# Attention, dense layer and routed experts in one kernel: routing logits in four column groups, shorter routing, weight splits and scores at other steps

## The chip, the cores and the metric

The kernel runs on one core of a Trainium2 chip. The metric is the time on the device in microseconds, as the median of several runs; the time before is 1757.74 us.

## What is computed

The reference, cut to what matters here (`a` below is the output of a two-step attention on packed keys, reshaped to 4608 tokens of 512 values):

```python
h = a @ w_in                        # 4608x512 by 512x2048
x = (h - tanh(h)) @ w_out           # 4608x512: the tokens that are routed
logits = x @ w_gate                 # 512x8
noise_scale = log1p(exp(x @ w_noise))
noisy = logits + noise_scale * noise
top2 = two largest of the 8 per token; weights = softmax over the two
for e in range(8):                  # for the tokens that chose expert e
    out[mask] += weight * (relu(x[mask] @ w1[e]) @ w2[e])
```

## The kernel before

The kernel has three phases. Phase A (about the first 150 us) makes the packed values of the attention. Phase B works on 16 chunks of 288 tokens (`TN`); a batch is two chunks. Phase C runs the experts on blocks of 128 gathered tokens: each block has 12 products of 512 columns for each half of `g1` (L1104) and 24 for `g2` (L1146).

Large products are made of three: both operands are split into a high part in `fp32r` and the rest (`split`, L97 on ACT and L101 on DVE), and high x high, high x low and low x high are added up in PSUM.

Phase B is a loop over 256 steps of 16 to a chunk (numbered 0 to 15 below). A step computes one 128-row piece of the hidden layer, `g1` (L475, 6 products into `h`), its tanh (L482 on ACT) and difference (L484 on DVE, `g`), the split of the piece of the step before into `gh` (L97) and `gl` (L101), and, three steps late, the second product `g2` (L500, 12 products into `acc`). So a step has 18 products of 288 columns. `h` has two PSUM buffers: the products of a step wait until `g` of two steps earlier is made. All other work is hung on these steps by a table (`todo`, filled by `at(t, f)`): at the end of a step its entries are issued in the order in which they were entered, and PE, ACT, DVE and SP run their instructions in the order of issue. POOL is ordered by the scheduler. The entries that matter here:

- `u_mm`, `u_hi`, `u_lo`: four times in an odd chunk, at steps 7, 9, 11 and 15, eight float32 products of 512 columns into `u` and their split.
- Scores of the next chunk (`Queries`): float32 products `sq` (L299), two transposes `st` on DVE, the maximum `mq` (L311), a subtraction on POOL (L315), exponential, sum `rq` (L324 to L326), a multiplication on POOL (L330), a transpose `a` and its split. They start at step 1 of each chunk.
- `rows` and `xsplit` at steps 3 to 6: a finished chunk `xr` is transposed into `row` (L515) for its store, and split into `xh` and `xl`.
- `logits` at step 7 or 13: 4 + 4 `fp32r` products into `lg` (L528, L530), copied to `lgs` (L532). The split of the gate weights stands beside them in 32 columns. `logits_t` one step later: three transposes into `lt` (L544), and an addition of the two halves into `lgt`.
- `route`, once for two chunks, in pieces over some 15 steps from step 9 of an even chunk: small DVE operations on 96x48 values: a polynomial (L583, L584), two maxima, and a running count of tokens for each expert (`Mc`, `msum`, L619, L620). `rank` at step 13 of the next odd chunk: two products (L629, L630); then `slots`, and 12 scatters on POOL.
- `load_w`, `split_w`, `store_w` for 128 pieces `wt` of the expert weights: 256 KB loaded by SP, split by ACT and DVE, 512 KB stored by SP. They were spread evenly, load 4 steps ahead of the split and store one step behind it. `wt` has four buffers, so a load waits for the store four pieces earlier. The steps of the splits:

```python
j = T0 + (217 - T0) * i // 128
at(max(T0 - 1, j - 2), load_w, i)
at(j + 2, split_w, i)
at(j + 3, store_w, i)
```

The PSUM pool `pm` (tag `m`, two buffers) is shared by `u`, `sq`, `lg`, `lt` and `rk`. The last chunk's split, logits and routing stand in the first blocks of phase C (`run`, through `L`).

Of the kernel before, what the change touches and what calls it, by code (L numbers as in the profile page):

```python
# [21 lines left out]
P = 128  # L22
# [329 lines left out]
def consts_b(K, pp, pq, zero, w_gate, w_noise):  # L352
# [14 lines left out]
    wraw = pp.tile([P, 4, 16], F32, name="wgraw")  # L367
    nc.sync.dma_start(wraw[:, :, :8], w_gate.rearrange("(c p) e -> p c e", p=P))
    nc.sync.dma_start(wraw[:, :, 8:], w_noise.rearrange("(c p) e -> p c e", p=P))
    K.wg = cp.tile([P, 4, 32], FR, name="wg")  # L370
    nc.vector.tensor_copy(K.wg[:, :, :16], wraw)
    nc.vector.tensor_tensor(K.wg[:, :, 16:], wraw, K.wg[:, :, :16].bitcast(F32), op=ALU.subtract)
# [18 lines left out]
def phase_b(K, stack, wo_stack, qT, w1, w2, w_out, wide_out, noise, w_gate, w_noise, out):  # L391
# [25 lines left out]
    with ExitStack() as ctx:  # L417
# [99 lines left out]
        def xsplit(ch, d):  # L517
            xr = XT[ch]
            if d == 0:
                RAW["xs", ch] = tuple(xp.tile([P, 4, TN], FR, tag=f"x{x}", name=f"x{x}{ch}") for x in "hl")  # L520
            xh, xl = RAW["xs", ch]
            split(K, xh[:, d], xl[:, d], xr[:, d], "act", "dve")
# [17 lines left out]
        def logits_t(ch):  # L540
            lgs = RAW.pop(("lgs", ch))
            lt = pm.tile([P, 512], F32, tag="m", name=f"lt{ch}")
            for i in range(3):
                nc.tensor.transpose(lt[:96, i * 32:(i + 1) * 32], lgs[:, i * 96:(i + 1) * 96], K.ident[:32, :32])  # L544
            if ch % 2 == 0:
                LG[ch // 2] = rt.tile([96, 6, 16], F32, tag="lg", name=f"lgt{ch}")
            z = LG[ch // 2][:, (ch % 2) * 3:(ch % 2) * 3 + 3, :]
            ltv = lt[:96, :96].rearrange("p (i n) -> p i n", i=3)
            nc.vector.tensor_copy(z, ltv[:, :, :16])
            nc.vector.tensor_tensor(z, ltv[:, :, 16:], z, op=ALU.add)  # L550
# [12 lines left out]
        def route(u):  # L563
# [52 lines left out]
            Mb, Mc = T("Mb", dt=BF), T("Mc", dt=BF)  # L616
# [6 lines left out]
            RT[u] = (Mb, Mc, m1, m2, o1, o2)  # L623

        def rank(u):
            Mb, Mc, m1, m2, o1, o2 = RT.pop(u)
            n = 8 * u[2]
            rk = pm.tile([P, 512], F32, tag="m", name=f"rk{u[0]}_{u[1]}")
            nc.tensor.matmul(rk[:96, :n], K.tri, Mb.rearrange("p i e -> p (i e)"), start=True, stop=False)  # L629
# [709 lines left out]
```

## Time and profile before

| | |
|---|---|
| runs | 1751.29, 1757.74, 1761.91 us, median 1757.74 |
| the profiled execution: its time, its span | 1761.15 us, 1759.4 us |
| mean granted TensorE clock | 0.959 of full speed |
| PE busy | 1634.9 us, 93% of the span |
| DVE busy | 1201.5 us, 68% |
| ACT busy | 880.8 us, 50% |
| POOL busy | 567.0 us, 32% |
| phase B's steps | 151.1 us to 855 us of the span |

Busy time of PE is the union of its products' spans, and products overlap, so a short wait of PE hides in it; the distance from the start of one product to the start of the next (0.13 us for 288 columns) is what tells them. "Idle before, releaser" at a row's end names the operation whose end let an engine go on.

### The profile page before, as it was taken

To read this page: it belongs to the slowest core of one execution; us is meant where nothing else is said; L and a number is where in the kernel's file an instruction comes from. 1 tells how busy PE (TensorE), PEld (TensorE's weight loads), DVE (VectorE), ACT (ScalarE), POOL (GpSimd) and SP (SyncE) were. 2 spreads that over 40 slices of the span, in tenths; PEclk is the share of its full clock that TensorE was granted. 3 is DMA by queue.
4 is the path that set the end of the run, shared out by engine and by line. 5 is a ranking of instruction groups with operands and counts; after the bars stand their busy time and mean duration, and the time that the engine had idled before them with its cause. 6 is when DMAs were issued, how large, how long until landed. Compare 5 with 4: busy or idle time off the path is not lost.

```text
span 1759.4 us, 29416 instructions
## 1 busy us (share of the span) xinstructions
PE 1634.9 (93%) x9944; PEld 1383.9 (79%) x9944; DVE 1201.5 (68%) x3113; ACT 880.8 (50%) x1876; POOL 567.0 (32%) x559
## 2 busy tenths in 40 slices
PE   5668999999999999999876899999999999999996
PEld 3335889898989898989765688888888888888885
DVE  7886978887878788967464566666666666666652
ACT  3454655555555555544252455555555555555552
POOL 0001200121212121122445544545444454545421
PEclk8677999999999999999898899999999999999998
DMA  8783367777767687833236665523663236722621
GB/s 273 239 273 102 113 215 238 220 244 209 245 208 240 207 246 213 249 76 111 82 81 254 214 214 164 149 49 81 207 235 53 49 81 207 239 49 48 213 57 26
DMA packets 145655, 293.60 MB, mean 167 GB/s; under 512 B 19682, under 2 KB 69130, under 8 KB 140380
## 3 DMA queue, kind: packets, MB, share of 16 engines
q1 hardware_dynamic: 121676, 252.17, 43.1%
q0 software_dynamic: 23824, 39.51, 12.3%
q8 instruction: 80, 1.31, 0.3%
q14 instruction: 75, 0.61, 0.1%
HBM read 687.34 MB, written 107.59 MB: 452 GB/s over the span
## 4 chain that ended last, share of the span: by engine, by line
PE 81%; DVE 10%; ACT 3%; issue 3%; DMA 1%; another core or an unknown queue 1%; POOL 0%; DVEq 0%; POOLq 0%; ACTq 0%
PE ph L1104 23%; PE py L1146 22%; PE acc L500 19%; PE h L475 10%; PE u L441 2%; PE s L175 2%; ACT ht L1126 1%; PE tp L199 1%; PE pv L211 1%; DVE xl L101 1%; DVE g L484 1%; PE sq L299 1%; DVE gl L101 1%; DVE nm L180 1%
## 5 line engine op out<-in xcount | busy, mean ns | idle before, releaser
L1104 PE MATMUL ph<-w0s,xh 128*128 128x512 f32 x1200 | 379.6, 398 | 19.5 <-ACT xh L97 12.9
L1126 ACT ACTIVATE ht<-h 32x256 f32<-32x256 f32 x624 | 259.8, 416 | 266.8 <-issue 139.2
L1146 PE MATMUL py<-w1s,hh 128*128 128x512 f32 x1200 | 373.0, 392 | 3.5 <-issue 3.4
L965 POOL DMA_INDIRECT x<-x1d,gidxm x276 | 265.0, 960 | 320.1 <-DVE xt L975 249.0
L500 PE MATMUL acc<-gh,wol 128*128 128x288 f32 x1024 | 302.7, 296 | 3.0 <-issue 3.0
L500 PE MATMUL acc<-gh,woh 128*128 128x288 f32 x1024 | 302.3, 295 | 2.2 <-issue 2.2
L500 PE MATMUL acc<-gl,woh 128*128 128x288 f32 x1024 | 301.8, 295 | 2.7 <-issue 2.7
L1106 DVE STREAM_TRANSPOSE h<-ph 128x512 f32<-128x512 f32 x150 | 107.3, 716 | 269.8 <-PE ph L1104 239.8
L1104 PEld LDWEIGHTS ph<-w0s,xh 128*128 128x128 f32 x1200 | 228.4, 191 | 72.2 <-ACT xh L97 13.9
L1146 PEld LDWEIGHTS py<-w1s,hh 128*128 128x128 f32 x1200 | 226.6, 189 | 55.1 <-issue 6.8
L1146 PE MATMUL py<-w1s,hl 128*128 128x512 f32 x600 | 235.6, 393 | 8.3 <-DVE hl L1135 6.1
L1104 PE MATMUL ph<-w0s,xl 128*128 128x512 f32 x600 | 238.7, 398 | 0.0
L665 POOL DMA_INDIRECT table<-d,qi x96 | 91.6, 954 | 386.9 <-DVE g L484 227.4
L500 PEld LDWEIGHTS acc<-gh,woh 128*128 128x128 f32 x1024 | 193.5, 189 | 4.8 <-issue 4.8
L500 PEld LDWEIGHTS acc<-gl,woh 128*128 128x128 f32 x1024 | 193.2, 189 | 2.4 <-issue 2.4
L500 PEld LDWEIGHTS acc<-gh,wol 128*128 128x128 f32 x1024 | 193.1, 189 | 1.6 <-issue 1.6
L97 ACT ACTIVATE gh<-g 128x288 fp32r<-128x288 f32 x256 | 113.5, 443 | 153.2 <-DVE g L484 150.2
L1124 DVE TENSOR_SCALAR ht<-h 32x256 f32<-32x256 f32 x576 | 178.5, 310 | 10.6
L475 PE MATMUL h<-a2h,uh 128*128 128x288 f32 x512 | 158.9, 310 | 7.5 <-DVE g L484 6.5
L482 ACT ACTIVATE t<-h 128x288 f32<-128x288 f32 x256 | 103.9, 406 | 113.0 <-PE h L475 94.3
L475 PE MATMUL h<-a2h,ul 128*128 128x288 f32 x512 | 151.6, 296 | 0.2 <-DVE ul L450 0.2
L475 PE MATMUL h<-a2l,uh 128*128 128x288 f32 x512 | 151.5, 296 | 0.0
(234 smaller groups left out, 2468.2 us busy)
## 6 DMA issues: line engine op xcount, KB each, us to landing
w0s<-wsp SPq DMA_DIRECT2D x140, 2048.0 KB
w1s<-wsp SPq DMA_DIRECT2D x140, 2048.0 KB
wsp<-wt SPq DMA_DIRECT2D x128, 512.0 KB
wt<-in_w_dram SPq DMA_DIRECT2D x128, 256.0 KB
kT<-in_kT_dram SPq DMA_DIRECT2D x16, 608.0 KB
out_dram<-zero SPq DMA_DIRECT2D x37, 256.0 KB
v<-in_v_dram SPq DMA_DIRECT2D x16, 576.0 KB
q<-in_qT_dram SPq DMA_DIRECT2D x32, 288.0 KB
```

What stands on the lines that cost most here:

```text
L97: nc.scalar.activation(hi, src, AF.Copy)
L101: e.tensor_tensor(lo, src, hi.bitcast(F32), op=ALU.subtract)
L475: nc.tensor.matmul(h[:, :TN], u[:, G, fs], x[:, G, :], start=(n == 0), stop=(n == 5))
L482: nc.scalar.activation(t, h[:, :TN], AF.Tanh)
L500: nc.tensor.matmul(ACC[ch][d][:, :TN], w[:, d * P:(d + 1) * P], x, start=(f == 0 and n == 0), stop=(f == 15 and n == 2))
L665: ins = nc.gpsimd.indirect_dma_start(out=K.table, out_offset=IO(ap=qi[:, i:i + 1], axis=0), in_=d[:, i, :], in_offset=None, oob_is_err=True)
L965: g = K.nc.gpsimd.indirect_dma_start(out=x[:, b, :], out_offset=None, in_=rows, in_offset=IO(ap=gidx[:, c, b:b + 1], axis=0))
L1104: K.nc.tensor.matmul(p, xx[:, d * P:(d + 1) * P], w[:, fc, ws, d, :], start=(n == 0), stop=(n == 11))
L1106: self.last = V.transpose(h[:, 2 * fc:2 * fc + 2].rearrange("p g n -> p (g n)"), p).ins
L1124: V.tensor_scalar(dst, src, 0.0, None, op0=ALU.max)
L1126: K.nc.scalar.activation(dst, src, AF.Relu)
L1146: K.nc.tensor.matmul(p, xx[:, f * P:(f + 1) * P], w[:, f // 4, ws, f % 4, :], start=(n == 0), stop=(n == 23))
```

## The change

The logits become four float32 products, one for each 128 rows of the contraction, that write four groups of 32 PSUM partitions from the unsplit `xr`; the three transposes become three float32 products with a matrix `fold` that adds the four groups up. The split of `x` goes away. The polynomial takes one operation for two. The running count over six rows is made by the ranking products instead (six more small products for each `rank`, less one) and one reduction. Scores start at step 4 instead of 1. Each entry of the table may carry a weight for DVE, and the splits of expert weights are put by a dynamic program on the 128 steps of least weight among 17 to 218, at most four in a row, with the load three steps ahead instead of four.

```diff
+    K.fold = cp.tile([P, 16], F32, name="fold")
+    nc.vector.tensor_reduce(K.fold, K.ident.rearrange("p (j n) -> p n j", n=16), axis=AX.X, op=ALU.add)
...
-    K.wg = cp.tile([P, 4, 32], FR, name="wg")
...
+    K.wg = cp.tile([P, 4, 32], F32, name="wg")
+    nc.vector.memset(K.wg, 0.0)
+    nc.sync.dma_start(K.wg[:, :, :8], w_gate.rearrange("(c p) e -> p c e", p=P))
+    nc.sync.dma_start(K.wg[:, :, 8:16], w_noise.rearrange("(c p) e -> p c e", p=P))
...
-        def xsplit(ch, d):
...
         def logits(ch):
-            xh, xl = RAW.pop(("xs", ch))
             lg = pm.tile([P, 512], F32, tag="m", name=f"lg{ch}")
             for d in range(4):
-                nc.tensor.matmul(lg[:32, :TN], K.wg[:, d, :], xh[:, d], start=(d == 0), stop=False)
-            for d in range(4):
-                nc.tensor.matmul(lg[:16, :TN], K.wg[:, d, :16], xl[:, d], start=False, stop=(d == 3))
-            lgs = RAW["lgs", ch] = rt.tile([32, TN], F32, tag="lgs", name=f"lgs{ch}")
-            nc.vector.tensor_copy(lgs, lg[:32, :TN])
+                nc.tensor.matmul(lg[32 * d:32 * d + 32, :TN], K.wg[:, d, :], XT[ch][:, d], start=True, stop=True)
+            lgs = RAW["lgs", ch] = rt.tile([P, TN], F32, tag="lgs", name=f"lgs{ch}")
+            nc.vector.tensor_copy(lgs, lg[:, :TN])
...
-                nc.tensor.transpose(lt[:96, i * 32:(i + 1) * 32], lgs[:, i * 96:(i + 1) * 96], K.ident[:32, :32])
+                nc.tensor.matmul(lt[:96, i * 16:(i + 1) * 16], lgs[:, i * 96:(i + 1) * 96], K.fold, start=True, stop=True)
...
-            V.tensor_scalar(acc, s2, 2.0 / 17, 2.0 / 15, op0=ALU.mult, op1=ALU.add)
-            for k in (13, 11, 9, 7, 5, 3):
-                V.tensor_tensor(acc, acc, s2, op=ALU.mult)
-                V.tensor_scalar(acc, acc, 2.0 / k, None, op0=ALU.add)
-                yield
-            V.tensor_tensor(acc, acc, s2, op=ALU.mult)
+            V.tensor_scalar(acc, s2, 2.0 / 17, None, op0=ALU.mult)
+            for k in (15, 13, 11, 9, 7, 5, 3):
+                V.scalar_tensor_tensor(acc, acc, 2.0 / k, s2, op0=ALU.add, op1=ALU.mult)
+                if k % 4 == 3:
+                    yield
...
-            for i in range(n):
-                V.tensor_copy(Mc[:, i], K.msum)
-                V.tensor_tensor(K.msum, K.msum, M[:, i], op=ALU.add)
-                if i % 2:
-                    yield
+            V.tensor_copy(ms, K.msum)
+            yield
+            V.tensor_reduce(Mc, M.rearrange("p i e -> p e i"), axis=AX.X, op=ALU.add)
+            V.tensor_tensor(K.msum, K.msum, Mc, op=ALU.add)
...
-            nc.tensor.matmul(rk[:96, :n], K.ones[:, :96], Mc.rearrange("p i e -> p (i e)"), start=False, stop=True)
+            for j in range(1, n):
+                nc.tensor.matmul(rv[:, j:], K.ones[:, :96], Mb[:, :n - j], start=False, stop=False)
+            nc.tensor.matmul(rv, K.ones[:, :96], ms.unsqueeze(1).to_broadcast([96, n, 8]), start=False, stop=True)
...
-            q = (4, 5, 5, 6, 7, 8, 9, 10, 11, 12) if ch == 1 else (1, 2, 2, 3, 4, 5, 6, 7, 10, 12)
-            at(0 if ch == 1 else w - 3, Q.load_q, ch)
+            q = (4, 5, 6, 7, 8, 9, 10, 11, 12, 13)
+            at(0 if ch == 1 else w - 1, Q.load_q, ch)
...
-                r, pace = {11: (18, 2), 13: (15, 1.25)}.get(ch, (27, 2.5))
+                r, pace = {11: (16, 2), 13: (15, 1.25)}.get(ch, (27, 2.5))
...
+        first, last = T0 + 2, 219
+        best = {(0, 0): (0, None)}
+        trail = []
+        for t in range(first, last):
+            w = sum(c * heavy.get(t + o, 0) for o, c in ((-1, 1), (0, 2), (1, 1)))
+            new = {}
+            for (n, r), (c, _) in best.items():
+                for take in (0, 1):
+                    if take and (r == 4 or n == 128):
+                        continue
...
+        for i, t in enumerate(reversed(at_w)):
+            at(max(T0 - 1, t - 3), load_w, i)
+            at(t, split_w, i)
+            at(t + 1, store_w, i)
...
-            for d in range(4):
-                L.split(d)
```

In most chunks the splits now stand at steps 1 to 4 and 6 to 9 of an even chunk, at 13 to 15, and at steps 1 to 4, 6, 7 and 9 of an odd one.

DVE in chunk 7, all that stood between `g` of step 6 and `g` of step 7 before (`Mc` and `msum` are the running count, `rq` the scores' sum, `xl` the split that goes away):

```order
L619 CAST Mc_0_6147<-msum 96x8
L620 TENSOR_TENSOR msum<-msum,M_0_6144 96x8
...
L324 TENSOR_REDUCE rq_6192<-st_6022 128x18
L325 TENSOR_SCALAR rq_6192<-rq_6192 128x18
L326 RECIPROCAL rq_6192<-rq_6192 128x18
L515 STREAM_TRANSPOSE row_6066<-xr_6006 128x9x32
L101 TENSOR_TENSOR xl_6069<-xr_6006,xh_6068 128x288
L101 TENSOR_TENSOR wt_6029<-wt_6029 128x512
L101 TENSOR_TENSOR gl_6_6204<-g_6_6174,gh_6_6203 128x288
L484 TENSOR_TENSOR g_7_6216<-h_7_6207,t_7_6214 128x288
```

The same place now, and on to `g` of step 8:

```order
L306 STREAM_TRANSPOSE st_6022<-sq_1_5979 128x288
L516 STREAM_TRANSPOSE row_5942<-xr_5887 128x9x32
L101 TENSOR_TENSOR wt_5947<-wt_5947 128x512
L101 TENSOR_TENSOR gl_6_6063<-g_6_6042,gh_6_6062 128x288
L485 TENSOR_TENSOR g_7_6075<-h_7_6066,t_7_6073 128x288
L311 TENSOR_REDUCE mq_6103<-st_6022 128x18
L101 TENSOR_TENSOR wt_5993<-wt_5993 128x512
L101 TENSOR_TENSOR gl_7_6114<-g_7_6075,gh_7_6113 128x288
L485 TENSOR_TENSOR g_8_6126<-h_8_6117,t_8_6124 128x288
```

Up to and with `g` of step 7 twelve operations stood there (the count's two rows stand there twice), and five do now; the sums `rq` have moved to four steps later, and the maximum `mq` stands after `g`.

PE, step 13 of chunk 3, where ranking (`rk`) and the logits of chunk 2 (`lg`) follow the step's last `acc`. Before:

```order
L629 LDWEIGHTS tri
L629 MATMUL rk_0_3891<-Mb_0_3559,tri 96x48
L630 LDWEIGHTS ones
L630 MATMUL rk_0_3891<-Mc_0_3560,ones 96x48
L528 MATMUL lg_3894<-xh_3481,wg 32x288 x4
L530 MATMUL lg_3894<-xl_3482,wg 16x288 x4
```

Now:

```order
L618 LDWEIGHTS tri
L618 MATMUL rk_0_3830<-Mb_0_3441,tri 96x48
L620 LDWEIGHTS ones
L620 MATMUL rk_0_3830<-Mb_0_3441,ones 96x40
...
L620 LDWEIGHTS ones
L620 MATMUL rk_0_3830<-Mb_0_3441,ones 96x8
L621 LDWEIGHTS ones
L621 MATMUL rk_0_3830<-ms_0_3442,ones 96x48
L522 MATMUL lg_3838<-xr_3391,wg 32x288 x4
```

Two ranking products have become seven, and eight logit products four.

## Rows read from the trace of the kernel before

**Rows 1.** Busy time in windows: first and last batch of chunks 2 to 13, sum.
```profile
core 0: us, PE busy (x) PEld busy (x) DVE busy (x) ACT busy (x) POOL busy (x), PEclk, DMA share, GB/s
248.30:335.50 87.20, 86.05 (x705) 79.68 (x697) 70.19 (x192) 48.57 (x115) 6.05 (x4) 1.00 0.72 231
...
687.60:774.00 86.40, 86.35 (x704) 79.83 (x696) 70.82 (x196) 45.69 (x111) 21.25 (x23) 1.00 0.68 198
sum 525.70, PE 520.40 PEld 478.85 DVE 423.19 ACT 286.71 POOL 97.17; mean PE 86.73 PEld 79.81 DVE 70.53 ACT 47.79 POOL 16.19
```

**Rows 2.** The same view: the shortest even chunk (2) and odd chunk (13).
```profile
248.30:288.80 40.50, 40.50 (x324) 39.43 (x317) 33.66 (x90) 23.82 (x57) 2.32 (x2) 1.00 0.75 240
728.40:774.00 45.60, 45.55 (x383) 40.26 (x381) 35.63 (x98) 22.15 (x55) 13.18 (x15) 1.00 0.64 180
```

**Rows 3.** Timeline of PE, step 8 to step 9 of chunk 7: start, us, what.
```profile
487.25 0.29 PE L500 MATMUL acc<-gh,wol 128*128 128x288 f32 x1
488.17 0.40 PE L475 MATMUL h<-a2h,uh 128*128 128x288 f32 x1 [0.62 <-DVE g L484]
```

**Rows 4.** Timeline of DVE just before that.
```profile
485.42 1.36 DVE L101 TENSOR_TENSOR xl<-xr,xh 128x288 fp32r<-128x288 f32 x1
486.70 0.68 DVE L101 TENSOR_TENSOR wt<-wt 128x512 fp32r<-128x512 f32 x1
487.30 0.45 DVE L101 TENSOR_TENSOR gl<-g,gh 128x288 fp32r<-128x288 f32 x1
487.67 0.45 DVE L484 TENSOR_TENSOR g<-h,t 128x288 f32<-128x288 f32 x1
```

**Rows 5.** Groups of instructions by line: count | busy us, mean ns | idle before.
```profile
L101 DVE TENSOR_TENSOR xl<-xr,xh 128x288 fp32r<-128x288 f32 x64 | 49.7, 779 | 7.1 <-ACT xh L97 7.1
L584 DVE TENSOR_SCALAR acc<-acc 96x48 f32<-96x48 f32 (+1 forms) x54 | 10.5, 195 | 1.9
L583 DVE TENSOR_TENSOR acc<-acc,s 96x48 f32<-96x48 f32 (+1 forms) x54 | 10.4, 193 | 0.7
L619 DVE CAST Mc<-msum 96x8 bf16<-96x8 f32 x48 | 8.2, 172 | 0.9
L620 DVE TENSOR_TENSOR msum<-msum,M 96x8 f32<-96x8 f32 x48 | 7.8, 164 | 1.7
```

**Rows 6.** Timeline of PE, step 13 of chunk 7: ranking, logits, next step.
```profile
503.25 0.19 PE L629 MATMUL rk<-Mb,tri 96*96 96x48 bf16 x1
503.28 0.20 PE L630 MATMUL rk<-Mc,ones 96*96 96x48 bf16 x1
503.33 0.69 PE L528 MATMUL lg<-xh,wg 128*32 128x288 f32 x4
503.85 0.70 PE L530 MATMUL lg<-xl,wg 128*16 128x288 f32 x4
504.39 0.29 PE L475 MATMUL h<-a2h,uh 128*128 128x288 f32 x1
```

**Rows 7.** Timeline of PE, chunk 3: the scores' float32 products, two instructions each.
```profile
293.39 0.29 PE L500 MATMUL acc<-gh,wol 128*128 128x288 f32 x1
293.61 0.72 PE L299 MATMUL sq<-q,pt 64*32 64x288 f32 x16
294.26 0.40 PE L475 MATMUL h<-a2h,uh 128*128 128x288 f32 x1
294.49 0.30 PE L475 MATMUL h<-a2l,uh 128*128 128x288 f32 x1
```

**Rows 8.** Timeline of PE: `logits_t` of one chunk.
```profile
506.62 0.29 PE L500 MATMUL acc<-gh,wol 128*128 128x288 f32 x1
506.85 0.33 PE L544 MATMUL lt<-ident,lgs 32*96 32x32 f32 x3
507.10 0.40 PE L475 MATMUL h<-a2h,uh 128*128 128x288 f32 x1
```

**Rows 9.** Timeline of PE: four float32 products of few columns, 128-column weights.
```profile
828.30 1.03 PE L924 MATMUL gpse<-toke,sel 128*128 128x6 f32 x8 [0.49 <-DVE gatee L917]
829.19 0.38 PE L475 MATMUL h<-a2h,uh 128*128 128x288 f32 x1
```

**Rows 10.** Timeline of PE, first blocks of phase C.
```profile
903.87 0.80 PE L1146 MATMUL py<-w1s,hl 128*128 128x512 f32 x1 [5.73 <-DVE hl L1135]
```

**Rows 11.** Timeline of SP's queue: two stores of weights, and the loads that follow them.
```profile
547.65 1.30 SPq L464 DMA_DIRECT2D wsp<-wt  x2
554.15 1.56 SPq L455 DMA_DIRECT2D wt<-in_w_dram  x2
```

More of the change, by code (lines that the diff above doesn't have):

```diff
@@ L547, in logits_t @@
             z = LG[ch // 2][:, (ch % 2) * 3:(ch % 2) * 3 + 3, :]
[L548 to L550 removed]
+            nc.vector.tensor_copy(z, lt[:96, :48].rearrange("p (i n) -> p i n", i=3))
         RT = {}
@@ L615, in route @@
             V.tensor_tensor(M, o1, o2, op=ALU.add)
[L616 removed]
+            Mb, ms, Mc = T("Mb", dt=BF), rt.tile([96, 8], BF, tag="ms", name=f"ms{b}_{i0}"), rt.tile([96, 8], F32, tag="Mc", name=f"Mc{b}_{i0}")
             V.tensor_copy(Mb, M)
[L618 to L623 removed]
+            V.tensor_copy(ms, K.msum)
+            yield
+            V.tensor_reduce(Mc, M.rearrange("p i e -> p e i"), axis=AX.X, op=ALU.add)
+            V.tensor_tensor(K.msum, K.msum, Mc, op=ALU.add)
+            RT[u] = (Mb, ms, m1, m2, o1, o2)
         def rank(u):
[L626 to L627 removed]
+            Mb, ms, m1, m2, o1, o2 = RT.pop(u)
+            n = u[2]
             rk = pm.tile([P, 512], F32, tag="m", name=f"rk{u[0]}_{u[1]}")
[L629 to L630 removed]
+            rv = rk[:96, :8 * n].rearrange("p (i e) -> p i e", e=8)
+            nc.tensor.matmul(rv, K.tri, Mb, start=True, stop=False)
+            for j in range(1, n):
+                nc.tensor.matmul(rv[:, j:], K.ones[:, :96], Mb[:, :n - j], start=False, stop=False)
+            nc.tensor.matmul(rv, K.ones[:, :96], ms.unsqueeze(1).to_broadcast([96, n, 8]), start=False, stop=True)
             RT[u] = (rk, m1, m2, o1, o2)
@@ L675, in phase_b, with at @@
         TOT = NCH * 16
-        todo = {}
-        def at(t, f, *args):
+        todo, heavy = {}, {}
+        def at(t, f, *args, w=0):
             todo.setdefault(t, []).append((f, args))
+            heavy[t] = heavy.get(t, 0) + w
         for b in range(1, NB):
@@ L688, in phase_b @@
                 for r in range(2):
-                    at(t + 1, u_lo, b, k, r)
+                    at(t + 1, u_lo, b, k, r, w=7)
         for ch in range(1, NCH):
             w = 16 * ch - 16
-            q = (4, 5, 5, 6, 7, 8, 9, 10, 11, 12) if ch == 1 else (1, 2, 2, 3, 4, 5, 6, 7, 10, 12)
-            at(0 if ch == 1 else w - 3, Q.load_q, ch)
-            for d, f in zip(q, (lambda c: Q.scores(c, pm, "m"), lambda c: Q.tr(c, 0), lambda c: Q.tr(c, 1),
+            q = (4, 5, 6, 7, 8, 9, 10, 11, 12, 13)
+            at(0 if ch == 1 else w - 1, Q.load_q, ch)
+            for d, m, f in zip(q, (0, 5, 5, 7, 8, 0, 12, 8, 7, 7), (lambda c: Q.scores(c, pm, "m"), lambda c: Q.tr(c, 0), lambda c: Q.tr(c, 1),
                                 Q.max, Q.sub, Q.exp, Q.sum, Q.mul, Q.out, Q.split)):
-                at(w + d, f, ch)
+                at(w + d, f, ch, w=m)
         for z in range(NPAD // P):
@@ L702, in phase_b @@
                 if ch < 15:
-                    at(te + 1 + d, rows, ch, d)
-                    at(te + 1 + d, xsplit, ch, d)
+                    at(te + 1 + d, rows, ch, d, w=4)
             slow = ch % 2 == 0 and ch < 14
@@ L707, in phase_b @@
                 continue
-            at(te + (11 if slow else 5), logits, ch)
+            at(te + (11 if slow else 5), logits, ch, w=4)
             at(te + 5, store_rows, ch)
-            at(te + (12 if slow else 6), logits_t, ch)
+            at(te + (12 if slow else 6), logits_t, ch, w=2)
             if ch % 2 or ch == 14:
@@ L714, in phase_b @@
                 at(te + 7, route, u)
+                for i in range(12):
+                    heavy[te + 8 + i] = heavy.get(te + 8 + i, 0) + 6
                 if ch == 14:
                     continue
-                r, pace = {11: (18, 2), 13: (15, 1.25)}.get(ch, (27, 2.5))
+                r, pace = {11: (16, 2), 13: (15, 1.25)}.get(ch, (27, 2.5))
                 at(te + r, rank, u)
-                at(te + r + 1, slots, u)
+                at(te + r + 1, slots, u, w=7)
+                heavy[te + r + 2] = heavy.get(te + r + 2, 0) + 14
                 for i in range(12):
@@ L749, in phase_b @@
             at(max(i, 5 + 12 * (i - NWA) // max(1, 15 - NWA)), split_wo, i)
-        for i in range(128):
-            j = T0 + (217 - T0) * i // 128
-            at(max(T0 - 1, j - 2), load_w, i)
-            at(j + 2, split_w, i)
-            at(j + 3, store_w, i)
+        first, last = T0 + 2, 219
[8 more added lines that the diff above has]
+                        continue
+                    k = (n + take, r + 1 if take else 0)
+                    v = c + take * w
+                    if k not in new or v < new[k][0]:
+                        new[k] = (v, (n, r))
+            trail.append(new)
+            best = new
+        k = min((k for k in best if k[0] == 128), key=lambda k: best[k][0])
+        at_w = []
+        for t in range(last - 1, first - 1, -1):
+            p = trail[t - first][k][1]
+            if p[0] < k[0]:
+                at_w.append(t)
+            k = p
+        for i, t in enumerate(reversed(at_w)):
+            at(max(T0 - 1, t - 3), load_w, i)
+            at(t, split_w, i)
+            at(t + 1, store_w, i)
         Q.split(0)
@@ L824, in scatters @@
             scatter(u, i)
-    L.split = lambda d: xsplit(15, d)
     L.rows = lambda d: rows(15, d)
```

10 lines of the change are left out of this document (removed).

## The prediction

> **What bounds the kernel now.** I read the share of busy time first (PE 93%, DVE 68%), then PE's timeline step by step in phase B, then the windows over its chunks. PE's busy time tells little, since it covers short waits: a batch is over 98% busy in the first and in the last window [rows 1]. What tells is the distance between starts. Products of 288 columns follow each other at 0.13 us, so 18 make a step of some 2.38 us, and a step that carries nothing else takes that. The shortest even chunk takes 40.50 us and the shortest odd one 45.60 us [rows 2], together 86.1. The six batches from chunk 2 to 13 take 525.70 us [rows 1], and six times 86.1 is 516.6: **9.1 us are lost in waits**. Where they lie: between the last product of step 8 and the first of step 9 in chunk 7 there are 0.92 us instead of 0.13, and the row names DVE's `g` [rows 3]. DVE had reached that `g` late because of what stood ahead of it, among it an `xl` of 1.36 us and a weight split of 0.68 us [rows 4]. The same `fp32r` subtraction of 288 columns takes 0.45 us as `gl` [rows 4], and the mean of all `xl` is 779 ns [rows 5]: the long ones overlap a pass of POOL over the scores, which begins as soon as the sum or the maximum is made. One more wait of the kind, 0.49 us, stands in chunk 15 [rows 9]. So phase B is bound by PE, with 9.6 us of late DVE on top; phase C's blocks are bound by PE throughout, except for the first ones, where PE waits 5.73 us for DVE once [rows 10].
>
> **DVE's load falls.** Removed are 64 `xl` (49.7 us), 54 of the 108 polynomial operations (54 of 0.19 us, 10.5 us), and most of the count: 96 operations of 16.0 us become 27 of about 0.17 us, 11 us less [rows 5]. That is 71 us over some 700 us, or about 9 us in a batch, where DVE was busy for 70.5 us of 87.6 [rows 1]. More weighs where it goes. Ahead of `g` of step 7 stood a list of 4 x 0.17 for the count, about 1.2 for the sum, 0.42 for the transpose, 1.36, 0.68, 0.45 and 0.45, together 5.2 us. Now it is two transposes of about 0.45, 0.68, 0.45 and 0.45: 2.5 us, where the step before it gives 2.4. A backlog that no longer grows to a step's length can't hold PE, which has two buffers of `h`. The wait at step 1 of even chunks, for PSUM buffers that the last `u` of the chunk before still holds, goes with the scores' move to step 4. I take 9.0 of the 9.6 us as recovered; from 4 to 9.6 is possible.
>
> **PE's own work stays about even.** Three edits change it, on the path in each case, since PE is the bound.
> - Logits. Before, eight products of 0.13 us: from 503.33 to 504.39, 1.06 us [rows 6]. No row has four float32 products of 128 rows in four column groups. The nearest are the scores: eight float32 products, 64 rows by 32 columns, in four column groups, 16 instructions. From the last `acc` to the second `h` it is 1.10 us, where two normal steps of 0.13 would be 0.26, so 0.84 us net [rows 7]. Each float32 product is two instructions, and the sixteen ran side by side: the whole group is 0.72 us long [rows 7]. Part of the 0.84 stands before the first product and behind the last (0.22 and 0.33 us instead of 0.13), and the logits of before, also 32 columns wide, paid neither [rows 6]. So between 0.55 and 0.84 if they run side by side. I take 0.75, nearest to the scores: 0.31 less, times 15 chunks, **4.6 us less**. The other end, one after another, is the first rival.
> - `logits_t`. Before: from the last `acc` to `h` 0.48 us, 0.35 more than normal [rows 8], three weight loads of 96 columns. Now six, since float32 takes two instructions for each product. Bounds for one more: 0.06 us, the pace inside the 0.33 us of three [rows 8], and 0.11 us, an eighth of the 0.89 us in which eight such instructions with 128 weight columns run [rows 9]. 96 columns scale the second to 0.083, which I take: six steps of it for three of 0.06 are 0.25 to 0.3 more, times 15, **4.1 us more** (2.5 to 6).
> - Ranking. Five more products in each of seven units, at 0.03 to 0.05 us by the two before [rows 6]: **1.3 us more**.
> The sum is 0.8 us more, from 5 less to 5 more.
>
> **What is moved at no cost, and its cover.** The scores' chain (first transposes, maximum, sum, `a`, its split) ends at step 13 instead of 12; the next chunk needs it at step 16, three steps or 7 us later. The load of `q` is issued at step 15 for use at step 4, 12 us. On SP it and the weight loads stand behind each other in order; a load that waits for a store holds the others, and all have steps of slack. The weight splits cost ACT and DVE what they cost before; what is new is that up to four follow each other at one step's distance (second rival). POOL's two passes keep their length, but the operations behind them change: behind the sum now stand `gl` and `g`, so `gl` will be the one that is held for about 0.9 us. PE needs `gl` two steps later, so that is covered too, as long as DVE is otherwise in time (third rival). The consts' few operations lie in the first steps, beside other waits.
>
> **Phase C's first blocks.** The last chunk's split goes, but PE waited there for nothing of it. Before `hl`, on which PE waits 5.73 us [rows 10], the routing is cut at another place: before it stopped after 15 operations behind the reciprocal, now after 19, about 0.2 us each, so 0.8 us more; logits and the saved addition bring some 0.5 us back. I set 0.3 us more. The expert blocks behind are the same instructions.
>
> **The sum.** 9.0 less, 0.8 more, 0.3 more: **7.9 us less**. The profiled execution took 1761.15 us and would take 1753.3; it lies 3.4 us above the median of the runs shown, which would become 1749.8. With the bounds of the terms, 4 to 9.6, 5 less to 5 more, and 1 for the first blocks, the forecast's own range is 1743 to 1756. About 0.5% (8.8 us) is what a measurement of this kernel can tell from no change, so the forecast straddles the bound of faster at 1748.9.
>
> **Rivals.**
> - *The four float32 products do not run side by side.* Then eight passes come one after another. From the first of the scores' products to the next `h` it is 0.65 us, in which each of the eight makes two passes, so a pass takes 0.33 us at most; eight make 2.6 us, 1.55 more than before instead of 0.31 less: 1.86 times 15, 28 us above the forecast: **1778 us** at most, slower. It decides from 1.3 us for one group on, where the loss eats what is left of the recovered waits. For it: the four share all 128 rows, the scores' products only 64. Against: 16 instructions fit into 0.72 us [rows 7], where one after another would take 2.1 us even at the 0.13 us of an `fp32r` product. The Trainium skill (TensorE: Matmul & The Clock Gate, Part 3, what overlaps and what doesn't) says that a weight load overlaps products in flight only where its row group differs, by which four column groups over the same rows would go one after another; this case's trace speaks against it so far, with four column groups of the same 64 rows inside the 0.72 us. Chance 0.07.
> - *Weights come late.* Four splits in a row leave a buffer five steps, 11.9 us, from split to split where the even spread left 6.3 steps. Of these DVE's part of the split and the step to the store take 3.1. A load was issued 5.2 us after the issue of two stores had ended [rows 11], and a load of half the bytes is at most as long, so that the two take up to 10.4 us of the 8.8 that are left. Where they are over, ACT waits for the load with `t` and `gh` behind it, and PE for both. One to two us in some five of the 26 bursts, 8 us in all: **1758 us**, no change. Chance 0.12.
> - *The waits move instead of going.* POOL's hold falls on `gl` and on the weight splits behind the maximum, with `u_lo` and the sum in the same steps of odd chunks. Half of the 9 us stay: **1754 us**. Chance 0.16.
> - *More is freed than rows show*: the steps of chunks 0 and 1, in which PE waits too, gain 3 us, and the logits take 0.55: **1743 us**. Chance 0.1.
>
> **Chances.** The forecast has 0.55. Faster by over 0.5%: somewhat under half of the forecast's 0.55 lies below 1748.9, since its middle lies just above; that is 0.25, and with the last rival's 0.1 and 0.05 of the two before it 0.4. Slower: the first rival's 0.07 and 0.01 of the second: 0.08. The rest, 0.52, is no change. The range that leaves out the first rival and the tails is 1742 to 1758.
>
> **What would show it.** In the changed profile the four `lg` products of a chunk end within 0.6 to 0.85 us; six `lt` instructions take 0.45 to 0.6 us. Batches of chunks 2 to 13 take 86 to 87 us each, odd step 8 ends in no wait, and the waits of PE for `g` and `ul` are under 1 us in sum. DVE's busy time falls from 1201 to about 1130 us, and ACT's by the splits of x. A group of `lg` over 1.3 us, ACT's `wt` waiting for its load, or batches above 88 us would prove the forecast wrong, each by its rival.

## The result and the profile after

The changed kernel takes 1740.8 us (median of 4 runs, 1736.05 to 1745.8) where the kernel before, beside it on the same chip, takes 1755.05 (median of 4 runs, 1751.29 to 1761.91; the 1757.74 from which the forecast counts is the median of three of them): ratio 0.9905, interval 0.9883 to 0.9926. Measured once more with the experiments it is 0.9891 (0.9876 to 0.9905), 19 us. The forecast was 1749.8 with a range of 1742 to 1758, so the gain was about twice the 7.9 us forecast (14 us in the first comparison, 19 in the second), and the measured time lies 1.2 us below the range.

The profiled execution after takes 1745.8 us, its span 1743.7, 15.6 less than before. Busy time on its page (us, share of the span, instructions):

```profile
PE 1627.6 (93%) x10031; PEld 1383.9 (79%) x10031; DVE 1140.2 (65%) x2910; ACT 860.2 (49%) x1812; POOL 565.5 (32%) x559
```

DVE has 61 us less to do, but PE is 93% busy as before; the shares say little of where the time went. Windows over the six batches from chunk 2 to 13, first, last and sum, with the columns of [rows 1]:

```profile
249.54:335.32 85.78, 85.78 (x716) 79.38 (x708) 62.33 (x166) 45.79 (x106) 4.67 (x4) 1.00 0.73 241
...
678.23:764.03 85.80, 85.80 (x709) 79.27 (x708) 63.17 (x172) 44.00 (x104) 22.10 (x24) 1.00 0.65 206
sum 514.49, PE 514.49 PEld 475.94 DVE 376.28 ACT 271.77 POOL 97.15; mean PE 85.75 PEld 79.32 DVE 62.71 ACT 45.29 POOL 16.19
```

Against 525.70 before: **11.2 us less**, every batch 85.7 to 85.8. The place of [rows 3], PE from the last product of step 8 to the first of step 9 in chunk 7, and DVE up to the `g` of that time, as in [rows 4]:

```profile
484.67 0.29 PE L501 MATMUL acc<-gh,wol 128*128 128x288 f32 x1
484.81 0.29 PE L476 MATMUL h<-a2h,uh 128*128 128x288 f32 x1
```

```profile
480.81 0.45 DVE L485 TENSOR_TENSOR g<-h,t 128x288 f32<-128x288 f32 x1
481.18 0.74 DVE L311 TENSOR_REDUCE mq<-st 128x18 f32<-128x576 f32 x1
484.48 0.69 DVE L101 TENSOR_TENSOR wt<-wt 128x512 fp32r<-128x512 f32 x1 [2.56 <-ACT wt L97]
485.09 0.45 DVE L101 TENSOR_TENSOR gl<-g,gh 128x288 fp32r<-128x288 f32 x1
485.46 0.45 DVE L485 TENSOR_TENSOR g<-h,t 128x288 f32<-128x288 f32 x1
```

0.14 us instead of 0.92, and DVE, which was late before, now stands idle for 2.56 us there, until ACT has made the high part of a weight split. Ranking and logits at step 13 of chunk 7, and `logits_t` in chunk 8 (before: [rows 6], [rows 8]):

```profile
499.20 0.19 PE L618 MATMUL rk<-Mb,tri 96*96 96x48 bf16 x1
499.23 0.37 PE L620 MATMUL rk<-Mb,ones 96*96 96x40 bf16 x5
499.45 0.20 PE L621 MATMUL rk<-ms,ones 96*96 96x48 bf16 x1
499.58 0.69 PE L522 MATMUL lg<-xr,wg 128*32 128x288 f32 x8
500.21 0.40 PE L476 MATMUL h<-a2h,uh 128*128 128x288 f32 x1
...
529.79 0.29 PE L501 MATMUL acc<-gh,wol 128*128 128x288 f32 x1
529.93 0.60 PE L536 MATMUL lt<-fold,lgs 128*96 128x16 f32 x6
530.38 0.38 PE L476 MATMUL h<-a2h,uh 128*128 128x288 f32 x1
```

The eight instructions of the logits fit into 0.69 us: the four column groups run side by side. In the trace four start within some 20 ns, and 0.25 us later the other four. The gain of phase B is there at the start of block 6 (969.38 before, 958.17 after). What came on top stands where the forecast put nothing: in the expert blocks. The same four stretches of blocks 19 to 21, from the first product of each half to the first of the next (`g1` of 20, `g2` of 19, `g1` of 21, `g2` of 20; columns of [rows 1]), before:

```profile
1134.83:1140.42 5.59, 5.59 (x25) 4.51 (x24) 2.06 (x5) 2.36 (x5) 4.33 (x4) 1.00 0.17 47
1140.42:1145.87 5.45, 5.45 (x25) 4.50 (x24) 4.71 (x11) 3.36 (x6) 1.09 (x2) 1.00 0.37 51
1145.87:1151.35 5.48, 5.48 (x26) 4.51 (x24) 2.15 (x5) 2.36 (x5) 4.40 (x4) 1.00 0.17 48
1151.35:1156.82 5.47, 5.47 (x25) 4.51 (x24) 4.71 (x11) 3.36 (x6) 0.98 (x1) 1.00 0.36 48
```

and after:

```profile
1125.38:1130.83 5.45, 5.45 (x26) 4.51 (x25) 2.16 (x5) 2.36 (x5) 4.37 (x4) 1.00 0.18 48
1130.83:1136.27 5.44, 5.44 (x26) 4.50 (x25) 4.71 (x11) 3.35 (x6) 1.08 (x2) 1.00 0.38 48
1136.27:1141.70 5.43, 5.43 (x25) 4.50 (x24) 2.18 (x5) 2.36 (x5) 4.39 (x4) 1.00 0.16 48
1141.70:1147.14 5.44, 5.44 (x25) 4.50 (x24) 4.72 (x11) 3.35 (x6) 1.07 (x2) 1.00 0.40 53
```

PE never waits in either, and the granted clock is full (1.00) in both. Yet the 24 products of `g1` take 5.59 us in an even block before, 5.45 after. In the trace they start some 232 and 235 ns apart in turn before, 227 after; in odd blocks of before only the first five to seven products of each half are slow. A block took 11.05 and 10.95 us in turn and now takes 10.88; the 64 blocks from 8 to 71 take 696.31 us instead of 703.78, **7.5 us less**, with the same instructions.

The two parts make 18.7 us, the spans differ by 15.6. The 3 us between them are in blocks 6 and 7. From block 6's first product to block 7's it is 25.5 us after and 20.7 before, with PE waiting for "issue", that is for nothing that the profile shows; block 7 gives 1.6 us of the 4.8 back. These waits differ between executions (last section), and the same kernel's later profile has 18.8 us in block 6.

### The profile page after: what moved, and what is told of

Same layout as the page of the kernel before. It is cut to its first block, busy times and chain, and to the rows that moved or that the text cites. A ratio compares the mean times of both kernels' runs of the same rounds, so it can differ in the third digit from the quotient of the medians.

```text
span 1743.7 us, 29334 instructions
## 1 busy us (share of the span) xinstructions
PE 1627.6 (93%) x10031; PEld 1383.9 (79%) x10031; DVE 1140.2 (65%) x2910; ACT 860.2 (49%) x1812; POOL 565.5 (32%) x559
## 4 chain that ended last, share of the span: by engine, by line
PE 86%; DVE 7%; ACT 2%; issue 2%; DMA 1%; POOL 1%; DVEq 0%; POOLq 0%; ACTq 0%
PE acc L501 23%; PE ph L1120 22%; PE py L1162 22%; PE h L476 12%; PE u L442 2%; PE s L175 2%; ACT ht L1142 1%; PE tp L199 1%; PE pv L211 1%; PE sq L299 1%; DVE cva L76 1%; PE lg L522 1%; DMA kT<-in_kT_dram 1%; DVE nm L180 1%; DVE cvf L88 0%
## 5 line engine op out<-in xcount | busy, mean ns | idle before, releaser
L656 POOL DMA_INDIRECT table<-d,qi x96 | 97.0, 1011 | 352.0 <-DVE g L485 270.5
L485 DVE TENSOR_TENSOR g<-h,t 128x288 f32<-128x288 f32 x256 | 115.8, 452 | 60.8 <-ACT t L483 56.3
```

The costliest lines, as they stand in the source:

```text
L485: PACE[0] = nc.vector.tensor_tensor(g, h[:, :TN], t, op=ALU.subtract).ins
L656: ins = nc.gpsimd.indirect_dma_start(out=K.table, out_offset=IO(ap=qi[:, i:i + 1], axis=0), in_=d[:, i, :], in_offset=None, oob_is_err=True)
```

## The experiments

Where the operands of phase C's products start is read from the built programs. The left-hand pools hold one slot of `w0s` (even blocks), both of `w1s`, `hh` and `hl`; the right-hand ones the other slot of `w0s` (odd blocks), the tokens `xh` and `xl`. Starts modulo 256 bytes, and the block lengths that the runs below showed:

```
kernel                       left   right   even, odd block (us)
before                        224       0   11.05  10.95
after                          32      32   10.88  10.88
1  after, right 32 lower       32       0   11.04  10.95
2  before, left 32 higher       0       0   10.88  10.88
3  after, xh, xl 32 lower      32      32*  11.04  11.04     * xh, xl: 0
4  after, even splits          32      32   10.88  10.88
5  after, scores of before     32      32   10.88  10.88
6  after, routing of before    32       0   11.04  10.95
7  after, logits of before    224      32   11.07  10.93
8  after, left 128 higher     160      32   11.05  10.90
9  before, scores, left 32      0       0   10.88  10.88
10 before, logits of after     32       0   11.04  10.95
11 before, splits of after    224       0   11.05  10.95
```

**1. The placement of before in the changed kernel.**

```diff
     rt = pool(K, stack, "b_rt", 1, side="right")
+    rt.tile([96, 8], F32, name="pad")
```

> The changed kernel with one unused tile of 32 bytes in the right-hand pool of the routing: the tables, one of the two slots of expert weights (w0s0) and the gathered tokens (x, xh, xl) lie 32 bytes lower, the rest as it was. No instruction differs. Theory (placement): in the kernel before, w0s0, xh and xl start at multiples of 64 bytes and the other operands of phase C's products 32 bytes beside one; after the change all of them start 32 bytes beside one, and that is why a block takes 10.88 us instead of alternately 11.05 and 10.95. Here the places modulo 64 are those of before, so blocks alternate between 11.05 and 10.95 us again, 0.12 us more on the mean, about 8 us in all over the changed kernel (ratio to the kernel before about 0.995 to 0.996 instead of 0.9905); chunks 2 to 13 keep 85.7 us a batch. Rival (phase B's end or the timing of the other engines sets the pace of the blocks): blocks stay at 10.88 us and the time at that of the changed kernel.

Measured: 0.9937 (0.9921 to 0.9952), 1740.18 against 1751.79 us. Blocks 11.04 and 10.95, the batches 514.9 us. An unused tile of 32 bytes takes back about 7.3 us (the 64 blocks from 8 on take 703.57 instead of 696.32), and it does so in the blocks alone; the ratio lies a little below the 0.995 expected, as the changed kernel itself stands nearer to 0.989 than to 0.9905.

**2. The placement of after in the kernel before.**

```diff
     K.quarter = cp.tile([P, 1], F32, name="quarter")
+    cp.tile([P, 8], F32, name="pad")
```

> The kernel before with one unused tile of 32 bytes among the constants: everything in the left-hand pools lies 32 bytes higher, so that all operands of phase C's products start at multiples of 64 bytes. No instruction differs. Theory (what counts is that moving and stationary operand start alike modulo 64 bytes): blocks take 10.88 us each, 7 to 8 us less in all (ratio to the kernel before 0.9955 to 0.996), and the batches of chunks 2 to 13 keep their waits, 525 to 526 us in sum. Rival 1 (what counts is the start itself, 32 beside a multiple of 64 being the good one): blocks at 11.05 us or more, the same time or slower. Rival 2 (the gain of the blocks has to do with the instructions or the timing): blocks as before, 11.05 and 10.95.

Measured: 0.9956 (0.994 to 0.9973), 1744.03 us. Blocks 10.88 and 10.88, batches 525.7 us in sum as before. So some 7.8 us (1744.03 against 1751.79) can be had from the kernel before by one line. Rivals 1 and 2 fall.

**3. The tokens alone.**

```diff
         self.xp = pool(K, stack, "c_x", 3, side="right")
+        self.xp.tile([P, 8], F32, name="pad", bufs=1)
```

> The changed kernel with one unused tile of 32 bytes beside the gathered tokens: only xt, xh and xl, the stationary operands of g1, lie 32 bytes lower, at multiples of 64 bytes; all four slots of expert weights stay 32 bytes beside one. Theory (moving and stationary operand must start alike modulo 64 bytes): the 24 products of g1 are slow in every block now, with both slots, by some 6.7 ns each, and with the change-overs every block takes about 11.05 us, 0.17 more than 10.88: some 12 us over the changed kernel (ratio to the kernel before about 0.997). If it is the place of the weights alone, or of the tokens alone by its distance to other tiles, blocks stay at 10.88 us.

Measured: 0.9969 (0.9959 to 0.998). The stretches of blocks 19 to 21, as above:

```profile
1114.46:1120.06 5.60, 5.60 (x26) 4.50 (x24) 2.07 (x5) 2.39 (x6) 4.36 (x4) 1.00 0.17 47
1120.06:1125.51 5.45, 5.45 (x26) 4.51 (x25) 4.71 (x11) 3.33 (x6) 1.09 (x2) 1.00 0.39 48
1125.51:1131.10 5.59, 5.59 (x26) 4.50 (x24) 2.10 (x5) 2.39 (x6) 4.39 (x4) 1.00 0.18 47
1131.10:1136.55 5.45, 5.45 (x26) 4.51 (x25) 4.71 (x11) 3.33 (x6) 1.09 (x2) 1.00 0.40 53
```

Now `g1` is slow with both slots, and `g2`, whose operands did not move, is not. It is the distance between the moving and the stationary operand that counts, as the theory said, with blocks of 11.04 us for the 11.05 expected.

**4. Weight splits spread evenly again.** The list of steps of the dynamic program is replaced:

```diff
+        at_w = [T0 + (217 - T0) * i // 128 + 2 for i in range(128)][::-1]
...
-            at(max(T0 - 1, t - 3), load_w, i)
+            at(max(T0 - 1, t - 4), load_w, i)
```

> The changed kernel with the weight splits spread evenly again, each load four steps ahead of the split and each store one behind it, as before the change; logits, routing and scores stay changed. Theory (waits of PE in chunks 2 to 13 come from a pile of DVE work ahead of g, and the shorter lists have removed most of it by themselves): between 0 and 4 of the 11 us come back, in odd chunks at steps that carry a row transpose, a split of u and a weight split together; batches 85.7 to 86.4 us. Rival (the placement of the splits in the lightest steps is what freed PE): 6 to 9 us come back, batches of 86.7 to 87.2 us. Blocks of phase C at 10.88 us in either case.

Measured: 0.9901 (0.9885 to 0.9917), 1734.2 us: no difference from the changed kernel that can be told. The batches:

```profile
588.01:674.46 86.45, 86.30 (x715) 79.38 (x707) 64.44 (x166) 45.62 (x107) 18.09 (x18) 1.00 0.78 229
674.46:761.38 86.92, 86.37 (x715) 79.39 (x707) 62.98 (x171) 43.71 (x103) 21.85 (x24) 1.00 0.68 204
sum 516.26, PE 515.56 PEld 475.95 DVE 379.63 ACT 271.91 POOL 97.86; mean PE 85.93 PEld 79.33 DVE 63.27 ACT 45.32 POOL 16.31
```

1.8 us come back, in the last two batches alone, and the time does not show them. The theory holds, the rival falls.

The base for 5 to 7 was **the changed kernel again**:

> The changed kernel once more, as the base for the three beside it on the same chip. By the sum of what the two kernels with 32 bytes of padding showed apart (0.9937 for all but the placement, 0.9956 for the placement alone) it should stand at 0.989 to 0.990 of the kernel before.

Measured: 0.9891 (0.9876 to 0.9905), batches 515.0, blocks 10.88.

**5. Scores at their old steps.**

```diff
-            q = (4, 5, 6, 7, 8, 9, 10, 11, 12, 13)
-            at(0 if ch == 1 else w - 1, Q.load_q, ch)
+            q = (4, 5, 5, 6, 7, 8, 9, 10, 11, 12) if ch == 1 else (1, 2, 2, 3, 4, 5, 6, 7, 10, 12)
+            at(0 if ch == 1 else w - 3, Q.load_q, ch)
...
```

> The changed kernel with the scores at their old steps again (from step 1, their query loaded three steps ahead); logits, routing and the places of the weight splits stay changed. Before the change PE waited 4.0 us in sum at step 1 of the even chunks among 2 to 13, where the scores wanted PSUM buffers that the last u still held, and 6.7 us at steps 8 and 9 of the odd ones. Theory (the scores' move is what took the wait at step 1 away): 3 to 4 us come back there, and up to 2 at odd steps 8, where the sum meets u again; batches 86.2 to 86.7 us, ratio 0.992. Rival (DVE's lighter lists alone took it away): under 1 us comes back. Blocks of phase C at 10.88 us.

Measured: 0.9911 (0.9897 to 0.9924); batches 517.8, that is 2.8 more than the base. PE at step 1 of chunk 8:

```profile
508.70 0.29 PE L501 MATMUL acc<-gh,wol 128*128 128x288 f32 x1
509.43 1.31 PE L299 MATMUL sq<-q,pt 64*32 64x288 f32 x16 [0.43 <-DVE ul L451]
510.67 0.40 PE L476 MATMUL h<-a2h,uh 128*128 128x288 f32 x1
```

and the same place in the kernel before:

```profile
515.40 0.29 PE L500 MATMUL acc<-gh,wol 128*128 128x288 f32 x1
516.12 1.31 PE L299 MATMUL sq<-q,pt 64*32 64x288 f32 x16 [0.43 <-DVE ul L450]
517.36 0.40 PE L475 MATMUL h<-a2h,uh 128*128 128x288 f32 x1
```

The wait for PSUM buffers until `ul` is made is back as it was, with the lighter lists of DVE. By the step lengths it is 3.7 us over six chunks (4.0 before the change). Nothing came back at odd steps 8 and 9. So the place of the scores makes this wait, as the forecast had it.

**6. The old routing** (polynomial, count and ranking as in the diff's minus lines).

> The changed kernel with the old routing: two operations for each term of the polynomial, the running count row by row on DVE, two ranking products instead of seven; the scatters and the rest stay changed. What is done for routing on DVE rises by some 21 us. Theory for phase B (any lighter DVE would do): 0 to 2 us of waits come back at odd steps 6 to 9, less 1.5 us for the ranking products: batches 85.5 to 85.9 us. Rival (the count ahead of g is what held PE at odd step 8): 3 to 5 us come back. Placement: the old count takes 32 bytes more in the routing's pool, so that the gathered tokens and one slot of weights start at multiples of 64 bytes again, and the other operands do not. By the placement theory blocks alternate between 11.04 and 10.95 us, 8 us more in all, without an instruction of theirs changed: ratio 0.993 to 0.995. If blocks stay at 10.88 us, it was another edit that moved them.

Measured: 0.9955 (0.9942 to 0.9969). Batches 515.0 us, as much as the base: most are up to 0.2 us shorter (85.52 against 85.72), the price of the ranking products, and chunk 13 has 1.3 us of waits more. Blocks 11.04 and 10.95: 703.57 us for the 64 from block 8 on, 696.32 in the base, 7.3 of the 8.5 us by which the spans differ (1744.3 and 1735.8); the medians are 12.0 us apart, and where the rest of that lies the profiles do not show. **So the 32 bytes that its smaller count frees are the larger part of what the routing edit brings**; in phase B the operations that it saves show in chunk 13 alone while the other edits stand, and the ranking products cost about as much again.

**7. The old logits** (`xsplit`, eight products, three transposes).

> The changed kernel with the old logits: x split into xh and xl, eight products in one column group, three transposes; routing, scores and the places of the weight splits stay changed. DVE has some 50 us more to do, ACT as well. PE's own work by the step lengths of the two profiles: 0.34 us more in each logits step, 0.22 less in each step of logits_t, 2 us more over 15 chunks. Theory (xl, long where POOL runs beside it, is what held g back): 4 to 7 us of waits come back at odd steps 6 to 9, batches 86.4 to 87.0 us, ratio 0.993 to 0.994. Rival (the other edits already leave room enough): under 2 us, batches 85.9 to 86.1. The padding-like shift here is 1024 bytes on the right and 64 on the left: if moving and stationary operand need only be alike modulo 64 bytes, blocks stay at 10.88 us; if modulo 128, they are slow with one slot, as before the change.

Measured: 0.9958 (0.9945 to 0.9971). Batches:

```profile
sum 516.79, PE 516.79 PEld 479.58 DVE 394.18 ACT 286.66 POOL 96.14; mean PE 86.13 PEld 79.93 DVE 65.70 ACT 47.78 POOL 16.02
```

1.8 to 2.3 us more, of which PE's own work is 1.4 (12 chunks of 0.34 less 0.22): here the rival was right, hardly a wait returns. Blocks 11.07 and 10.93, 7.7 us over the base in the 64 from block 8 on, which is most of the 12.3 us by which the medians differ; yet all starts are alike modulo 64 bytes, so 64 is not the measure.

**8. A distance of 128 bytes.**

```diff
     K.quarter = cp.tile([P, 1], F32, name="quarter")
+    cp.tile([P, 32], F32, name="pad")
```

> The changed kernel with one unused tile of 128 bytes among the constants: the left-hand operands (one slot of w0s, both of w1s, hh, hl) lie 128 bytes higher, the right-hand ones as they were. The run with the old logits had left-hand and right-hand operands alike modulo 64 bytes, 64 apart modulo 128, and its blocks were slow with one slot (11.07 us) and near the change-overs (10.93). If it is the start modulo 128 that must agree, blocks stay at 10.88 us here; if modulo 256 or more, they alternate between 11.05 to 11.07 and 10.93 to 10.95 us.

Measured in a single execution: 1752.96 us, blocks 11.05 and 10.90. So 128 is not enough either. In all these kernels the operands of a fast pair lie a multiple of 256 bytes apart, and those of a slow one do not (table above).

**9. Two small edits to the kernel before**: the scores' steps of the change, `11: (16, 2)` for its ranking, and the 32 bytes of experiment 2.

> The kernel before with two small edits: the scores at the later steps of the change (and one rank two steps earlier, which they need), and an unused tile of 32 bytes among the constants, which makes the operands of phase C's products start alike. Logits, routing and weight splits as before the change. Blocks: 10.88 us, 7.7 us less in all. Phase B, theory (the scores' place made both waits: the one at step 1 of even chunks for PSUM buffers, and by the sum of step 6 with POOL's pass behind it the one at steps 8 and 9 of odd chunks): of the 11 us lost in chunks 2 to 13 no more than 2 or 3 are left; ratio 0.990 to 0.992, as far as the whole change comes. Rival (the pile-up at odd steps 8 and 9 is made by xl, the count and the weight splits as well): only the 4 us of step 1 go, ratio 0.993 to 0.994.

Measured: 0.992 (0.9907 to 0.9934). Last batch and sum:

```profile
677.11:765.60 88.49, 87.11 (x704) 79.95 (x697) 68.43 (x196) 45.53 (x111) 21.89 (x24) 1.00 0.66 199
sum 518.30, PE 516.70 PEld 478.21 DVE 409.96 ACT 285.22 POOL 98.00; mean PE 86.12 PEld 79.70 DVE 68.33 ACT 47.54 POOL 16.33
```

Of the 11.2 us 3.8 are left, 2.7 of them in the last batch. There PE waits for `g` at the ends of steps 0 and 1 of chunk 13:

```profile
720.58 0.40 PE L476 MATMUL h<-a2h,uh 128*128 128x288 f32 x1 [0.45 <-DVE g L485]
724.14 0.40 PE L476 MATMUL h<-a2h,uh 128*128 128x288 f32 x1 [0.93 <-DVE g L485]
```

Between the two `g` that end these waits DVE runs eleven small operations of the old routing (0.16 to 0.21 us each, four of them the count), a weight split and `gl`, so that the `g` start 3.6 us apart where a step gives 2.4. With experiment 6, where the old routing alone brings 1.3 us of waits to chunk 13, this says that the routing's list is what holds PE there; taking it out of this kernel was not tried. In chunks 3 to 9 DVE is nearly as busy as before (410 and 423 us over the six batches), and still PE has no wait of that kind: moving the scores is enough, the load need not fall. The whole change is at 0.9891; some 14 of its 19 us come from these lines.

**10. The new logits alone.**

> The kernel before with the new logits alone: float32 products in four column groups from the unsplit x, three float32 products with fold, no xh and xl; scores, routing and weight splits as before the change. Placement: right-hand operands at multiples of 128 bytes, left-hand ones 32 beside, so blocks alternate as before the change (11.04 and 10.95 us). Phase B, theory (xl was one of several things ahead of g, enough of them to matter): of the 6.7 us lost at steps 8 and 9 of odd chunks at least 4 go, the 4 us of step 1 stay, and PE's own work falls by 0.1 us a chunk: batches 86.2 to 86.8 us, ratio 0.996 to 0.997. Rival: less than 2 us go, ratio 0.9985 or more.

Measured: 0.9936 (0.9922 to 0.9949), more than expected. Batches:

```profile
sum 516.79, PE 515.59 PEld 475.22 DVE 405.19 ACT 273.43 POOL 95.06; mean PE 85.93 PEld 79.20 DVE 67.53 ACT 45.57 POOL 15.84
```

8.9 us less than before: the 6.7 us at odd steps 8 and 9 go but for some tenths, and 1.4 us of PE's work; the step-1 waits (3.8 us) stay. In this profile block 6 starts 11.1 us earlier than before, so phase C's first blocks gained about 2 us too; why stays open.

**11. The new places of the weight splits alone.**

> The kernel before with the weight splits alone at the steps, and the loads and stores at the distances, of the change; logits, routing and scores as before. Theory (the places do nothing by themselves: the even spread in the changed kernel cost nothing either, and at steps 6 to 8 of odd chunks, where DVE is late, splits stand in the new places too): the waits stay between 9 and 14 us, ratio 0.998 to 1.002, blocks 11.05 and 10.95 us. Rival (the lightest steps free DVE where it is late): 5 us or more of waits go, ratio 0.997 or less.

Measured: 1.0023 (1.0009 to 1.0037), 4 us slower. PE from step 8 to step 9 of chunk 7 (0.62 us of idle time in [rows 3]), and the batches:

```profile
490.59 0.40 PE L475 MATMUL h<-a2h,uh 128*128 128x288 f32 x1 [1.11 <-DVE g L484]
...
sum 529.96, PE 523.21 PEld 479.05 DVE 423.29 ACT 287.25 POOL 98.24; mean PE 87.20 PEld 79.84 DVE 70.55 ACT 47.87 POOL 16.37
```

4.3 us more waits, 15.5 in all where the theory had 9 to 14: with the old scores the places are not light. By itself this part does harm; with the others it saves 1.8 us of waits at most (experiment 4), which the time does not show.

No version was found that beats the changed kernel by more than a measurement tells; experiment 4 equals it with less code.

## Why the prediction was wrong

- **The step that failed**: "The expert blocks behind are the same instructions", from which I set their change at nothing. They are the same, and the 64 from block 8 on took 7.5 us less, because the change shifted the tiles on which they work. Experiments 1, 2, 3 and 6 show it. Nothing in the change aimed at this, so that part of the gain is luck: `fold` lifts the left-hand operands by 64 bytes, the smaller count the right-hand ones by 32, and the two, 32 bytes apart before, now agree modulo 256. `fold` without the smaller count leaves them 32 bytes apart (6 and 10), the count without `fold` 64 (7). I had read no row on the blocks' pace, though the trace of before showed it: equal products some 232 to 235 ns apart in one block and mostly 227 in the next. Without this term the same forecast holds: experiment 1, the change with the old placement, is 0.9937, 11 us, inside the forecast's own range.
- **Waits**: 9.0 us taken as recovered, 11.2 measured for chunks 2 to 13, so this term was 2.2 us too small. All went; the waits of PE for `g` that are left, 1.8 us, lie in chunks 0 and 1. The floor of 86.1 us a batch came from two chunks that still had some tenths of waits; a batch without any takes 85.7, which is 2.1 us over six.
- **Their cause** was half right. The wait at step 1 went with the scores' move (experiments 5 and 10). For step 8 I named the list ahead of `g`; either of two edits alone takes that wait away, the scores (9) or the logits (10), so neither is needed once the other is made. That is why undoing one part (4 to 7) brings 0 to 3 us back and not its share. The 71 us less on DVE (61 measured) did not decide it: experiment 9 keeps nearly all of DVE's work and loses two thirds of the waits.
- **PE's own work**: 0.8 us more forecast. Logits: 0.73 us net taken from the step lengths (3.11 against 2.38), 0.75 forecast, 0.34 less than before, 5.1 us in 15 chunks (4.6). `logits_t`: 0.22 more a chunk, 3.3 us (4.1). Ranking: 0.2 to 0.22 for each unit, 1.5 us (1.3). Together 0.3 less; each within its bounds. Two of the sums were off, with no part in the miss: six times 0.083 less three times 0.06 is 0.32 us, 4.8 and not 4.1 in all, and the bounds as named (4 less, 5 more, 1 more) end the range at 1759.7, not at 1756.
- **Moved at no cost**: right. No wait of PE for `gl` or for the scores' `a` appeared; the first two chunks gained nothing (98.0 against 97.2 us), so the last rival, at 1743 us, came near the measured time for a wrong reason: its 3 us in those chunks did not come, and it had nothing for the blocks. Phase C's first blocks: within 0.6 us of no change.
- **Rivals**: the first is refuted, 0.69 us for the group. The rule of the Trainium skill that spoke for it (TensorE: Matmul & The Clock Gate, Part 3, what overlaps and what doesn't), that a weight load overlaps products in flight only where its row group differs, does not hold here: by it the groups would have followed one another, and by the rows all eight weight loads and products of the same 128 rows fit into 0.69 us. The second is there as a mechanism and not as a price. Among ACT's waits after (us in total, times, longest):

```profile
ACT wt L97 <- DMA wt<-in_w_dram: 17.4, 17, 2.5
```

  Before there was no such wait. ACT stands for late loads as that rival said, but no wait of PE for it appeared, and the even spread of experiment 4, where this wait is 5.3 us, is neither faster nor slower. Moved waits (the third) did not show.

## What to carry to other kernels

Read the pace of the steady part too, not only its waits: equal instructions that start at two different distances are a cost, and a change of any tile's size can move it. After a change of pools compare where the operands of the hottest products start, and test with an unused tile of 32 bytes: an edit's gain may be its placement. Undoing parts one by one undercounts waits that two parts remove; do each part alone as well.

## What the runs showed of the hardware

- The pace of `fp32r` products of 512 columns depends on how far apart the moving and the stationary operand start in SBUF: 226.7 ns from start to start when the distance is a multiple of 256 bytes, some 233 ns at distances of 32, 64 or 128 bytes from such a multiple (thirteen kernels, no exception; other distances were not tried). In the kernel before, a change between pairs at different places costs about 5 to 7 slow products as well, 0.03 to 0.04 us for a half block (5.48 against 5.44); with the pairs 64 bytes apart (experiment 7) it is three to ten, with 128 (experiment 8) one to three. The cause inside the chip stays open. The Trainium skill (TensorE: Matmul & The Clock Gate, Part 2, step-by-step) says that the two operands have read ports of their own, so that loading the next weights takes nothing from a running product; by that the distance would not matter, and the runs show that it does. For products of 288 columns no such difference was seen: `acc` products whose `wol` lies 64 bytes off (12 of the 16 pieces) start 131 to 133 ns apart like the others.
- Eight float32 instructions over the same 128 rows in four column groups take 0.69 us, nearly what 16 over 64 rows take (0.72 in [rows 7]).
- PE waits for "issue", with nothing late that the profile shows, at the end of phase B and about block 6: 13.4 us in the profile before, 22.2 and 21.8 in the two of the changed kernel, 11 to 22 in those of experiments 5 to 11, none in those of 1 to 4, which ran on one chip (the kernel before took 1751.8 us beside them, 1757.5 and 1760.2 beside 5 to 7 and 8 to 11). So it goes with the execution or the chip, not with the edit, and spans of two profiles are to be compared stretch by stretch. After, at the end of phase B:

```profile
851.84 0.29 PE L501 MATMUL acc<-gl,woh 128*128 128x288 f32 x1 [1.02 <-issue]
853.94 0.29 PE L501 MATMUL acc<-gh,wol 128*128 128x288 f32 x1 [1.81 <-issue]
855.33 0.40 PE L501 MATMUL acc<-gh,woh 128*128 128x288 f32 x1 [1.09 <-issue]
```
